# A Fourier mixing layer and an ELU feed-forward on one core: Z on two partition ranges, weights cast by their transfers, bias by matmul, three PSUM tiles for X

## The chip, the core and the metric

The kernel runs on one core of a Trainium2 chip. The core has a matrix engine, TensorE (PE in the profile; its weight loads are shown as PEld), and three engines for elementwise work: VectorE (DVE), ScalarE (ACT) and GpSimd (POOL). SyncE (SP) issues transfers; GpSimd issues some too. TensorE reads SBUF, the on-chip memory with 128 partitions, and writes PSUM, of which there are eight banks of 128 partitions by 512 f32. The other engines move results from PSUM to SBUF ("evict" them). Transfers between SBUF and DRAM run on 16 DMA engines that all queues share.

The metric is the device time of one execution in microseconds (us), as the median of several runs. Before the change it is 906.97 us, with runs from 906.8 to 907.77.

## What is computed

Shapes: x is 8 x 3008 x 256 (batch, sequence, features), w_r and w_i are 256 x 256, moe_w_in is 256 x 2048, moe_w_out is 2048 x 256; all are f32.

```python
X = np.fft.rfft(x, axis=1)
Yr = Xr @ w_r - Xi @ w_i + b_r
Yi = Xr @ w_i + Xi @ w_r + b_i
Yr = np.sign(Yr) * np.maximum(np.abs(Yr) - 0.01, 0.0)     # Yi likewise
y = np.fft.irfft(Yr + 1j * Yi, n=3008, axis=1)
h = y.reshape(24064, 256) @ moe_w_in
g = np.where(h > 0, h, np.exp(np.minimum(h, 0)) - 1)
out = g @ moe_w_out
```

## The kernel before

The sequence length is 47 x 64, so each Fourier transform is done in two small ones, as matmuls with tables of sines that the kernel computes itself in its first 22 us. One batch passes through these units:

- **A** (six units, `unit_A`): x times the table M1, two matmuls of 128x512. The result is evicted as bf16 and stored to DRAM (`DA`). All six stores of a batch must be there before any of it is read back.
- **Z** (`load_Z`, L172): DA is read back in another layout, 96 rows (24 x 2 x 2) on partitions 0 to 95, with 32 slots of 256 features in each row. A group is 8 slots. Batch 0 reads its four groups by four transfers; every other batch by two, one of slots 0 to 7 and one of slots 8 to 31.
- **X** (eight units, `unit_X`): unit u takes group u // 2 of the slots and half u % 2 of the features, eight matmuls of 96 columns against the table M2, which has one set of 96 rows for each slot. The result is evicted into XT by L126 (VectorE) or L128 (ScalarE).
- **M** (twelve groups, `m_group`): XT times the weights. wcat_r holds w_r beside w_i, and wcat_s holds -w_i beside w_r, both in bf16. Four matmuls of 128x512 make a group; then comes the bias and the soft threshold. In batch 0 (`first_M`) the groups alternate between two ways: in one, VectorE adds bias_bc (the bias on all partitions) and GpSimd applies the threshold; in the other, an extra matmul of a tile of ones (`busy`) with bias_p puts the bias into PSUM, where bias_p holds the bias as three bf16 pieces in rows 0, 32 and 64, and ScalarE and VectorE apply the threshold.
- **B** (six units) with the table M3, a store to DRAM (`DB`), a read back (`load_Bs`), and **Y** (eight units) with the table M4, which gives yT, the input of the feed-forward.
- The feed-forward: `front` multiplies a block of 512 tokens by w_in_s, ScalarE takes the exponential, VectorE and GpSimd finish the ELU as gT, and `back` multiplies by w_out_r and stores the output.

The order is written out by hand on every engine (`tc.manual_schedule`): the order in the source is the order of the engine's queue, and each engine works strictly through it. After batch 0's start the feed-forward of one batch runs interleaved with the units A to Y of the next two (`plan`). The first ten blocks (`FILL`) use a PSUM layout of their own, and with them run batch 1's last A units and batch 0's last Y units; batch 1's X units follow.

The start of batch 0 is what the change touches. In order:

- Biases: six small transfers (L441) put the two rows of the bias into `brow`, later VectorE and ScalarE split them into the bf16 pieces of bias_p (L747 to L756). Two further transfers spread the bias over all partitions (L666).
- Tables on VectorE and ScalarE: `points`, `phases`, `wraps`, `signs`, `sizes`, `sines` make M2 group by group.
- `idle_pe(n)` issues n matmuls on a tile of ones, whose results nobody reads: 9 at the start, 3 after each A unit, 40 after the last one, one after each X unit.
- Weights: w_r and w_i come in f32 on SP's queue (L657, L658), and GpSimd makes wcat_r and wcat_s by four operations (L659 to L662).
- `gate(Z_of[0][:, 8, 0:1])` is a tiny GpSimd copy that waits for Z's second group. Behind it in GpSimd's queue stand the transfers of batch 1's x (`load_x`, three of 1 MiB) and of half of w_out (1 MiB). A second such gate stands before batch 2's x.
- w_in comes in four f32 quarters on SP's queue (`load_w_in`, L717), into tiles that the feed-forward needs later (`Et`, `osb`). VectorE scales each by 2/S and casts it to bf16 in two halves (`scale_w_in`, L727), between the M units and in the first blocks of FILL.
- PSUM in the A and X stages: two tiles of two banks each (`pre2`) for the units and four of one bank (`pre1`), which the M groups use then.

## Time and profile before

The profile is of one execution on the chip. That execution took 911.15 us; the span from its first to its last instruction is 909.3 us. Its mean granted TensorE clock is 0.993 of full speed.

| what | value |
|---|---|
| median of three runs | 906.97 us (906.8 to 907.77) |
| the profiled execution, its span | 911.15 us, 909.3 us |
| VectorE: eight scalings of w_in (L727) | 5.2 us, 655 ns each |
| VectorE: bias split (L748, L753 to L756) | 3.3 us |
| SP: issues of Z, all batches (L172) | 18 |
| TensorE: X matmuls (L183), 96 rows x 96 columns | 512, 206 ns in the median |
| TensorE: fillers of `idle_pe` in the first 90 us | 70, 20.8 us |
| DMA moved in the whole span | 106.06 MB, 117 GB/s in the mean |

The durations of matmuls overlap, since they are pipelined; how fast they follow one another is read from the count in a stretch of the chain. The granted clock is given by stretches: 1.00 is full speed, 0.50 is half. A wait is put down to the last thing that released the waiting instruction. "Chain of waits" is the chain of work that ended last, followed back from the last instruction, at each step to what released it.

### The profile page before, as it was taken

How to read it: one execution, taken by the hardware profiler on the slowest of the kernel's cores; microseconds unless marked ns; L12 is line 12 of the kernel's file. 1: busy time of each engine (PE TensorE's matmuls, PEld its weight loads, DVE VectorE, ACT ScalarE, POOL GpSimd, SP SyncE). 2: the span in 40 equal slices, each digit the busy share in tenths (PEclk: the TensorE clock that was granted, in tenths of full speed). 3: DMA queues.
4: the chain of work that ended last, by engine and by line, in shares of the span. 5: the costliest groups of instructions: out<-in, count | busy, mean ns of one | idle time of the engine just before them, and what ended most of it. 6: DMA issues, size and time to landing. Idle time of an engine off the chain costs nothing.

```text
span 909.3 us, 17311 instructions
## 1 busy us (share of the span) xinstructions
PE 887.4 (98%) x6664; PEld 654.4 (72%) x6767; DVE 719.7 (79%) x908; ACT 696.1 (77%) x869; POOL 325.1 (36%) x457
## 2 busy tenths in 40 slices
PE   8898999999999999999999999999999999999997
PEld 3467667876678766886678766787667867777776
DVE  8687778887788778897788877888778877778776
ACT  6577778778878778787787788878887877767664
POOL 7552441233321341405404154032332134443665
PEclk9799999999999999999999999999999999999999
DMA  8977225721283214732266032752228011231011
GB/s 270 296 216 237 74 71 157 238 70 48 70 243 128 71 47 136 195 112 76 64 194 200 26 93 60 210 172 62 78 65 237 25 43 51 73 91 48 24 47 47
DMA packets 90655, 106.06 MB, mean 117 GB/s; under 512 B 5302, under 2 KB 81340, under 8 KB 87212
## 3 DMA queue, kind: packets, MB, share of 16 engines
q1 hardware_dynamic: 84316, 77.42, 30.5%
q0 software_dynamic: 5968, 27.26, 9.0%
q8 instruction: 53, 0.87, 0.4%
q10 hardware_dynamic: 288, 0.26, 0.1%
q14 instruction: 30, 0.25, 0.1%
HBM read 55.12 MB, written 49.81 MB: 115 GB/s over the span
## 4 chain that ended last, share of the span: by engine, by line
PE 85%; DVE 4%; ACT 3%; DMA 3%; issue 2%; POOL 1%; SPq 0%; DVEq 0%; ACTq 0%; POOLq 0%
PE ps_o L945 34%; PE hps L871 33%; PE mps L200 9%; PE bps L252 2%; PE yps L420 2%; PE xps L183 2%; PE aps L150 2%; DMA Z<-DA 1%; DVE gT L915 1%; DVE Et L926 1%; ACT Et L889 1%; ACT Et L892 1%; DMA xt<-in_x_dram 1%; ACT Bz L265 1%; DMA Bs<-DB 0%
## 5 line engine op out<-in xcount | busy, mean ns | idle before, releaser
L945 PE MATMUL ps_o<-w_out_r,gT 128*128 128x256 f32 x3008 | 475.3, 301 | 0.7 <-DVE gT L913 0.7
L945 PEld LDWEIGHTS ps_o<-w_out_r,gT 128*128 128x128 f32 x3008 | 402.9, 189 | 49.8 <-DVE osb L957 1.4
L871 PE MATMUL hps<-yT,w_in_s 128*128 128x512 bf16 (+7 forms) x1613 | 371.9, 350 | 5.9 <-DVE gT L913 1.0
L913 DVE SCALAR_TENSOR_TENSOR gT<-Et,hps 128x512 fp32r<-128x512 f32 (+1 forms) x268 | 220.2, 851 | 74.4 <-POOL Et L924 38.1
L915 DVE SCALAR_TENSOR_TENSOR gT<-hps,Et 128x1024 fp32r<-128x1024 f32 x190 | 232.4, 1223 | 14.9
L871 PEld LDWEIGHTS <-w_in_s 128*128 128x128 bf16 x1728 | 141.8, 98 | 129.0 <-issue 21.5
L924 POOL TENSOR_SCALAR Et<-Et 128x512 f32<-128x512 f32 x204 | 121.5, 615 | 230.9 <-ACT Et L887 218.6
L892 ACT ACTIVATE Et<-hps 128x1024 f32<-128x1024 f32 x190 | 195.8, 1031 | 9.7 <-PE hps L871 3.5
L926 DVE TENSOR_SCALAR Et<-Et 128x1024 f32<-128x1024 f32 x190 | 131.5, 692 | 47.9 <-ACT Et L892 40.4
L218 POOL TENSOR_SCALAR clip<-yb 128x512 f32<-128x512 f32 x84 | 51.7, 615 | 314.5 <-DVE yb L210 282.3
L887 ACT ACTIVATE Et<-hps 128x512 f32<-128x512 f32 x182 | 98.9, 595 | 62.4 <-PE hps L871 60.9
L889 ACT ACTIVATE Et<-hps 128x1024 f32<-128x1024 f32 x84 | 86.3, 1027 | 71.5 <-PE hps L871 70.0
L219 POOL TENSOR_TENSOR Y<-yb,clip 128x512 bf16<-128x512 f32 x84 | 107.2, 1277 | 7.0
L890 ACT ACTIVATE Et<-Et 128x1024 f32<-128x1024 f32 x84 | 88.8, 1058 | 2.6
L210 DVE TENSOR_TENSOR yb<-mps,bias_bc 128x512 f32<-128x512 f32 x89 | 61.3, 689 | 37.2 <-PE mps L200 24.8
L128 ACT CAST XT<-xps 128x768 bf16<-128x768 f32 x61 | 48.8, 799 | 17.9 <-PE xps L183 17.9
L200 PE MATMUL mps<-wcat_r,XT 128*128 128x512 bf16 x180 | 56.7, 391 | 0.8 <-ACT Bz L265 0.3
L200 PE MATMUL mps<-wcat_s,XT 128*128 128x512 bf16 x182 | 55.9, 385 | 0.7
L200 PEld LDWEIGHTS <-XT 128*128 128x128 bf16 x384 | 31.2, 99 | 30.9 <-issue 2.7
L128 ACT CAST A<-aps 128x1024 bf16<-128x1024 f32 x42 | 42.5, 1014 | 13.1 <-PE aps L150 11.7
L128 ACT CAST yT<-yps 128x752 bf16<-128x752 f32 x56 | 44.2, 789 | 10.4 <-PE yps L420 10.3
L265 ACT CAST Bz<-bps 128x1024 bf16<-128x1024 f32 x45 | 45.1, 1001 | 2.7 <-PE bps L252 2.7
(146 smaller groups left out, 466.7 us busy)
## 6 DMA issues: line engine op xcount, KB each, us to landing
xt<-in_x_dram POOLq DMA_DIRECT2D x21, 1024.0 KB, 7.1
out_dram<-osb SPq DMA_DIRECT2D x158, 128.0 KB
Bs<-DB SPq DMA_DIRECT2D x30, 384.0 KB
DA<-A SPq DMA_DIRECT2D x20, 512.0 KB
DB<-Bz SPq DMA_DIRECT2D x20, 512.0 KB
Z<-DA SPq DMA_DIRECT2D x7, 1152.0 KB
Z<-DA SPq DMA_DIRECT2D x11, 384.0 KB
xt<-in_x_dram POOLq DMA_DIRECT2D x6, 512.0 KB, 5.9
```

The costliest lines, as they stand in the source:

```text
L128: nc.scalar.copy(dst, src)
L200: nc.tensor.matmul(ps, lhsT=XT[:, dt, c, o : o + P], rhs=wm[:, dt, :], start=(not biased and m == 0 and dt == 0), stop=(m == 1 and dt == 1),)
L219: nc.gpsimd.tensor_tensor(Y_of[b, q][:, i, :], yb, clip[:], ALU.subtract)
L871: nc.tensor.matmul(hps[s][:, c0:c1] if early else hps[:, s, c0:c1], lhsT=w_in_s[:, dt, ft * P : ft * P + P], rhs=yT_of[b][:, dt, t0 : t0 + ...
L887: nc.scalar.activation(E_[:, s], hps[:, s], AF.Exp)
L889: nc.scalar.activation(E_, hps[:], AF.Relu, scale=-1.0)
L892: nc.scalar.activation(E_, hps[:], AF.Exp)
L913: nc.vector.scalar_tensor_tensor(o, e, -1.0, h, ALU.add, ALU.max)
L915: nc.vector.scalar_tensor_tensor(o, h, 0.0, e, ALU.max, ALU.add)
L924: nc.gpsimd.tensor_scalar(E_[s], E_[s], 1.0, 0.0, ALU.min, ALU.max)
L926: nc.vector.tensor_scalar(E_, E_, 1.0, -1.0, ALU.min, ALU.add)
L945: nc.tensor.matmul(po[q][:, i_ % 2, :], lhsT=gT[:, s, i_ * P : i_ * P + P], rhs=w_out_r[:, ft, :], start=(ft == 0 and i_ % 2 == 0), stop=( ...
```

## The change

It has six parts.

- **Z.** One tile Z0 of 128 partitions serves all batches. Groups 0 and 2 lie on partitions 0 to 95 as before, groups 1 and 3 on partitions 32 to 127. The X matmuls of groups 1 and 3 contract over all 128 partitions, of which the lower 32 of Z0 are cleared once (`clear`, ScalarE). M2 and its tables are computed on 128 partitions, with two sets of per-partition columns (`n=2`), one for each range. Every batch reads Z by four transfers, one for each group.
- **Weights.** GpSimd's queue loads w_r and w_i straight into the bf16 tile wcat_r, behind a gate that waits for the last A tile of batch 0; GpSimd makes wcat_s from it by two operations.
- **w_in.** GpSimd's queue loads it whole, 2 MiB, straight into the bf16 tile w_in_s, ahead of batch 1's x. `load_w_in` and `scale_w_in` are gone. The factor 2/S goes into w40 and w41, and with them into M4. The gates wait for Z's fourth group.
- **Bias.** Two transfers load it as 8 x 64, GpSimd makes the three bf16 pieces there, one transfer stores them to DRAM and three load them into rows 0, 32 and 64 of bias_p. A matmul of ones with bias_p gives the bias on all partitions, and ScalarE evicts it as bias_bc between X units 1 and 3.
- **PSUM.** In the A and X stages there are three tiles of two banks and two of one bank; for the M stage the pools are closed and opened again as two and four. Units 2, 4 and 7 of X are evicted by VectorE (before: 1, 4 and 7).
- **Order.** In batch 0 an M group takes both products of the first half of the features before those of the second. `idle_pe` after the last A unit is 34 matmuls instead of 40, and three instead of eight in the X stage. w3's subtraction moves behind X unit 2, a3 behind X unit 7.

The diff, cut to its core:

```diff
-    M2 = constp.tile([2 * NR, NS, 2, 2 * K1], BF16, name="M2")
+    M2 = constp.tile([P, NS, 2, 2 * K1], BF16, name="M2")
...
-    pre2 = first.enter_context(tc.tile_pool(name="pre2", bufs=2, space=bass.MemoryType.PSUM))
-    pre1 = first.enter_context(tc.tile_pool(name="pre1", bufs=4, space=bass.MemoryType.PSUM))
+    pre2 = zeroth.enter_context(tc.tile_pool(name="pre3", bufs=3, space=bass.MemoryType.PSUM))
+    pre1 = zeroth.enter_context(tc.tile_pool(name="pre0", bufs=2, space=bass.MemoryType.PSUM))
...
-        nc.sync.dma_start(Z_of[b][:, s0:s1, :], dv[:, s0:s1, :])
+        for g in range(s0 // 8, s1 // 8):
+            r, gs = 32 * (g % 2), slice(8 * g, 8 * g + 8)
+            nc.sync.dma_start(Z0[r : r + 2 * NR, gs, :], dv[:, gs, :])
...
+            r = slice(0, P if g % 2 else 2 * NR)
             nc.tensor.matmul(
-                psv[:, kk, 0 : 4 * K1], lhsT=Z[:, k, dt * P : dt * P + P],
-                rhs=M2[:, k].rearrange("p c m -> p (c m)"), start=True, stop=True,
+                psv[:, kk, 0 : 4 * K1], lhsT=Z[r, k, dt * P : dt * P + P],
+                rhs=M2[r, k].rearrange("p c m -> p (c m)"), start=True, stop=True,
             )
...
+        todo = [(c, dt) for c in range(2) for dt in range(2)]
+        if b == 0:
+            todo.sort(key=lambda z: z[1])
...
+    def gate(src):
+        t = gatep.tile([P, 1], F32, name="gate", tag="gate")
+        nc.gpsimd.tensor_copy(t[0 : src.shape[0], :], src)
...
+        def clear(g):
+            nc.scalar.activation(
+                Z0[0:32, 8 * g : 8 * g + 8, :].rearrange("p s d -> p (s d)"),
+                busy[0:32, 0:1].to_broadcast([32, 8 * D]), AF.Copy, scale=0.0,
+            )
...
+        for k in range(3):
+            pool.tensor_copy(bps[:, k], bsm[:])
+            if k < 2:
+                pool.tensor_tensor(bsm[:], bsm[:], bps[:, k], ALU.subtract)
...
-        wc = col(pool, wn, 1.0, ALU.add)
+        wc = col(pool, wn, 1.0, ALU.add, 2.0 / S, ALU.mult)
...
-        nc.sync.dma_start(w_r_f[:], w_r.rearrange("(c p) e -> p c e", p=P))
-        nc.sync.dma_start(w_i_f[:], w_i.rearrange("(c p) e -> p c e", p=P))
-        pool.tensor_copy(wcat_r[:, :, 0:D], w_r_f[:])
-        pool.tensor_copy(wcat_r[:, :, D : 2 * D], w_i_f[:])
-        pool.tensor_scalar(wcat_s[:, :, 0:D], w_i_f[:], -1.0, None, ALU.mult)
-        pool.tensor_copy(wcat_s[:, :, D : 2 * D], w_r_f[:])
+        gate(A_of[0, 2][:, 7, 0:1])
+        for o, wv in ((0, w_r), (D, w_i)):
+            nc.gpsimd.dma_start(
+                wcat_r[:, :, o : o + D], wv.rearrange("(c p) e -> p c e", p=P)
+            )
+        pool.tensor_copy(wcat_s[:, :, D : 2 * D], wcat_r[:, :, 0:D])
+        pool.tensor_scalar(wcat_s[:, :, 0:D], wcat_r[:, :, D : 2 * D], -1.0, None, ALU.mult)
+        for k in range(3):
+            nc.sync.dma_start(bias_p[32 * k : 32 * k + 1, :], bpd[k : k + 1, :])
...
-        idle_pe(40)
+        idle_pe(34)
...
-    load_w_in(0)
-    gate(Z_of[0][:, 8, 0:1])
+    gate(Z_of[0][:, 28, 0:1])
+    nc.gpsimd.dma_start(w_in_s[:], w_in_v)
     for ci in range(3):
         load_x(1, ci)
     load_w_out(0)
...
-    nc.vector.tensor_tensor(rest[:], brow[:], bias_p[:], ALU.subtract)
+    nb = pre1.tile([P, 512], F32, name="ips", tag="mps1")
     for u in range(8):
-        unit_X(0, u, alone=True, on_dve=u in (1, 4, 7))
+        unit_X(0, u, alone=True, on_dve=u in (2, 4, 7))
+        if u == 0:
+            nc.tensor.matmul(nb[:], lhsT=busy[:, 0:P], rhs=bias_p[:], start=True, stop=True)
         if u == 1:
-            nc.scalar.activation(a3[:], w3[:], AF.Abs)
-            nc.vector.tensor_copy(bias_p[32:64], rest[32:64])
-            nc.vector.tensor_copy(bias_p[64:P], rest[64:P])
-            nc.vector.tensor_tensor(rest[64:P], rest[64:P], bias_p[64:P], ALU.subtract)
-            nc.vector.tensor_copy(bias_p[64:P], rest[64:P])
-        idle_pe(1)
+            nc.scalar.copy(bias_bc[:], nb[:])
+        if u == 2:
+            nc.vector.tensor_tensor(w3[:], v3[:], w3[:], ALU.subtract)
+        if u in (1, 3, 5):
+            idle_pe(1)
+    nc.scalar.activation(a3[:], w3[:], AF.Abs)
+    zeroth.close()
...
-    scale_w_in(0, True, 0)
...
-            f1[xs[0]].append((lambda: gate(Z_of[1][:, 16, 0:1]), ()))
+            f1[xs[0]].append((lambda: gate(Z_of[1][:, 28, 0:1]), ()))
```

## The prediction

> **What bounds the kernel now.** I read the page first: its busy rows and its chain by engine.

> ```profile
> span 909.3 us, 17311 instructions
> PE 887.4 (98%) x6664; PEld 654.4 (72%) x6767; DVE 719.7 (79%) x908; ACT 696.1 (77%) x869; POOL 325.1 (36%) x457
> PE 85%; DVE 4%; ACT 3%; DMA 3%; issue 2%; POOL 1%; SPq 0%; DVEq 0%; ACTq 0%; POOLq 0%
> ```

> The matmuls set the end. From about 84 us on they run without a gap worth naming, so the eight batches behind the start cost what they cost, and a change of the start is passed to the end one for one. That leaves the first 84 us, which I read as the chain of waits from 20 to 40 us (start, length, what):

> ```profile
> 22.14 0.86 DVE A L745
> ...
> 23.90 1.10 DVE yb L748
> 25.00 0.88 DVE XT L126
> ...
> 25.92 0.68 PE xps L183 x8
> ...
> 28.77 0.81 ACT XT L128
> ...
> 31.53 0.97 DVE XT L126
> 32.55 1.46 PE mps L200 x3
> ...
> 34.23 2.94 PE mps L200 x8
> 37.16 0.22 PE mps L197
> 37.38 1.73 PE mps L200 x8
> ```

> VectorE is late, not the transfers: the second X unit waited for its eviction at 25.00 because the bias split (L748) stood ahead of it, and with two PSUM tiles the fourth unit waited behind it until 25.92. The same eight M matmuls that take 2.94 us at 34.23 take 1.73 at 37.38. The view by stretches says why (start:end, length, then busy time and count of PE, weight loads, VectorE, ScalarE, GpSimd; granted clock, DMA share, GB/s):

> ```profile
> 19.30:22.70 3.40, 3.40 (x24) 1.69 (x22) 3.37 (x8) 2.07 (x5) 3.40 (x3) 1.00 0.92 253
> 22.70:26.10 3.40, 1.64 (x28) 1.19 (x26) 3.33 (x5) 2.33 (x3) 3.34 (x5) 1.00 1.02 253
> 26.10:29.50 3.40, 3.06 (x27) 2.04 (x25) 2.98 (x5) 1.52 (x2) 1.86 (x3) 0.50 1.07 345
> 29.50:32.90 3.40, 3.07 (x20) 1.67 (x20) 1.34 (x2) 2.44 (x4) 0.00 (x0) 0.50 1.05 414
> 32.90:36.30 3.40, 3.18 (x8) 1.21 (x8) 2.13 (x3) 0.12 (x1) 1.39 (x2) 0.50 1.08 405
> 77.30:80.70 3.40, 2.39 (x27) 1.92 (x26) 1.23 (x3) 1.86 (x3) 0.00 (x0) 1.00 1.01 258
> ```

> After a stretch in which the matmuls were busy 1.64 of 3.40 us the clock is half for 10.2 us; a stretch with 2.39 of 3.40 did not cost it. Last, the timeline where the second batch's Z arrives (the bracket is the engine's idle time and what ended it):

> ```profile
> 77.11 0.52 PE L183 MATMUL xps<-M,Z 96*128 96x96 bf16 x8 [0.40 <-DMA Z<-DA]
> 83.63 0.52 PE L183 MATMUL xps<-M,Z 96*128 96x96 bf16 x8 [0.95 <-DMA Z<-DA]
> ```

> **The X stage: bias off VectorE, a third PSUM tile.** Removed from VectorE between 23.9 and 28.2: L748 1.10, L753 0.42, L754 0.42, L755 0.69, L756 0.70, 3.33 us in all. Added: one matmul (0.22 us, the step of L197 on the chain) and one ScalarE eviction of 128x512 f32 (0.59, the row of L957). The eviction of unit 1 moves to ScalarE, of unit 2 to VectorE. Laid out by the rows (a unit 0.50 at full clock, ScalarE 0.80, VectorE 0.95, Z's groups 1.4 us apart as 22.28 and 23.70 were): unit 1 evicted by 24.6, bias by 25.2, unit 2 on VectorE 24.3 to 25.3, w3 (0.96) to 26.2, unit 4 to 27.2, units 6 and 7 on PE by 27.7, unit 7 evicted at 28.75. First M matmuls 28.0 for the half of XT that is there (the new order), the rest from 28.8, instead of 31.7 and 32.5.

> In the stretch of 22.7 to 26.1 the matmuls then have units 0 to 4, the bias and one filler, some 2.6 of 3.4 us, above the 2.39 that kept the clock; with 34 instead of 40 fillers (0.226 each) the stretch before falls from 3.40 to about 2.5, also above. I take full clock. Then M runs at 0.86 a group and 1.08 with bias: (3,0) to 29.2, (3,1) to 30.3, (4,0) to 31.1, so (4,1) begins at 31.1 where it began at 37.0. One thing holds back: M3 needs a3 (0.84), two sines (0.85, 0.93) and two VectorE steps (0.96, 0.95), with an add of 0.69 between, done at 31.9, and Y(3,1) at 33.4 when B(3) could start at 33.1. **Term: 37.0 - 31.1 - 0.4 = 5.5 us**, about 3 of it waits and 2.5 clock.

> [...]

> **w_in by a casting transfer.** Removed: four SP transfers and eight scalings (L727, 8 x 0.655 = 5.2 us on VectorE). Two stand on the chain of waits, 0.55 at 44.34 and 0.69 at 61.55; the others lie beside the matmuls. **Term: 1.2 us.** Added: one transfer of 2 MiB on GpSimd's queue, ahead of x(1) and half of w_out, and a gate that opens at Z's fourth group instead of its second, 1 us later. Before, 4.5 MiB after the gate took from 24.5 to 38.9, 3.1 us a MiB with the rest of Z; 6 MiB so take 18.5 us, to about 44. Needed: first x tile at 46.5, w_out at 51.5 (51.99 and 56.98 less 5.5), so this is covered by 7 us; without cover each late us is one lost. What it meets: the last DB store (about 40) and the Bs load (48.41 less 5.5). The Bs data was there at 51.1, used at 52.5, 1.4 us of cover. I put 0 to 1.5 us and **take 0.5 lost**. No row shows a cast: nearest are x's transfers (7.3 us for 1 MiB to landing, all at the read's bytes) and, far off, the stretch 19 to 20 us, where the 1 KB rows of w_r and w_i moved 84 GB/s. I take the first, as these are 8 KB rows; the other is the rival on the other side.

> **w_r, w_i and the bias pieces on GpSimd.** GpSimd gains five ops of 8x64 (0.19 to 0.58 by L632 and L458; I take 1.2 us together, 2.9 at most), a gate and two issues (0.68 each), and loses two casts. Its issue of w_r moves from 15.48 (SP) to about 16.6, beside Z's first bytes: Z later by 0 to 1 us, **taken as 0.3**. wcat_s then costs 0.6 to 3.1 an op (L659 to L662), done by 20.5 to 27 against M at 28; at the top ends the gate behind it in the queue opens at 29, which eats 3.5 of the 7 us cover. SP's bpd store stands ahead of two DA stores, but its data is ready near 12 and the fifth store goes at 14.2: nothing. The three bias_p loads take the place of two weight loads (1.0 us of SP), while SP waits for DA until 18.4.

> **Edits at nothing.** Two clears of 32x2048 on ScalarE (0.8 to 2.0 each by L128's 128x768 and 128x1024): the first pushes the sine at 3.76 by 0.5 at most, covered by VectorE's 0.85 us idle ahead of 12.86; the second ends before A at 6.85. Two memsets (0.10) ahead of x's first issue: **0.2 lost**. M2 on 128 instead of 96 rows and a contraction of 128: same columns, same time (weight loads 98 ns for 96 and 128 rows alike in the rows). Fourteen more Z issues on SP (0.4 each, 18 becomes 32): SP waits 295 us for osb alone.

> **Batch 1's Z.** 1152 KB in one piece landed at 83.63, 6.5 us behind the first; as three, the second group lands near 79.3 at the same rate, before unit 2 could start (82.7). **Term: 0.95 us**, 0 at least if the pieces share their bytes, 1.3 at most with unit 0's wait.

> **Sum.** 5.5 + 1.2 + 0.95 - 0.5 - 0.3 - 0.2 = 6.65 us. The profiled execution took 911.15 us (span 909.3 and 1.85 around it), so 904.5 there; it stands 4.2 us above the median of the runs, 906.97, which gives 900.3.

> **Rivals.** (1) *Half clock anyway*, 0.20: X and M are dense sooner, but the clock falls near 26.1 and returns near 36.3. Units 6 and 7 then end at 28.1 (0.85 each), (3,0) at 29.9, (3,1) at 32.1, (4,0) at 33.8, (4,1) near 35.9, where before it ended at 38.1: 2.2 us instead of 5.5, sum 3.35, 903.6 us. For it: the dense stretches 26.1 to 32.9 did not bring the clock back. Against: 2.39 busy kept it.
> (2) *The gain is caught by the Bs chain*, 0.12: M ends early, but DB stores and Bs share the transfers' engines with w_in, x and w_out until 44 and past. If each of three steps (last store, Bs, its use) loses 1.5 us, 4.5 - 1.4 of cover = 3.1 more is lost beside the 0.5: 903.4. Against: 40 to 50 us has a DMA share of 0.51.
> (3) *A slow cast*, slower than before, 0.09: at 84 GB/s w_in takes 25 us instead of 6.2, w_out lands at 63 instead of 51.5, the first ps_o waits 11.3 us, net 11.3 - 6.65 = 4.7 worse: 911.7. It decides from 14 us for w_in (stall begins) and loses on the whole from 21 us, 100 GB/s.
> (4) *No more than the VectorE work*, 0.06: Z comes later than laid out (no gap of 1.4 us) and the X stage ends at 32 as now: only 1.2 us and noise, 905.8 to 907.

> **How the numbers follow.** My forecast has 0.53. Its own range is 898.5 (Z's wait at its top, contention none) to 902.3. 0.2% is 1.8 us, about what a measurement of this kernel can tell from no change. Faster: 0.53 + 0.20 + 0.12 = 0.85, less 0.02 for the far ends of (1) and (2); same 0.07; slower 0.10. The range 897.5 to 906.0 leaves out (3) and the tails.

> **What would show it.** Right: granted clock 1.00 in all stretches from 19 to 40 us; first XT eviction after 24.3 on VectorE without L748 ahead; M matmuls from 28; no PE wait for Z in units 2 and 3 of batch 1; FILL some 6 us earlier; the tail from there of equal length. Wrong: a clock of 0.50 between 26 and 36, PE waiting for w_in_s, xt or w_out_r, or Bs landing later than its use.

## The result, and the profile after

The changed kernel takes 912.83 us in the median (910.8 to 913.5), beside 907.66 us (906.8 to 908.13) for the kernel before on the same chip. The ratio is 1.0056 with a 95% interval of 1.0043 to 1.0069: slower by 0.56%, about 5.1 us. The forecast was 900.3 us, in a range from 897.5 to 906.0.

The profiled execution took 912.54 us. First the busy rows and the chain by engine of its page:

```profile
span 910.8 us, 17287 instructions
...
PE 883.6 (97%) x6654; PEld 652.8 (72%) x6757; DVE 712.2 (78%) x896; ACT 700.4 (77%) x871; POOL 325.7 (36%) x466
...
PE 86%; DVE 3%; issue 3%; ACT 3%; POOL 2%; DMA 2%; SPq 0%; DVEq 0%; ACTq 0%; POOLq 0%
```

VectorE lost its 7.5 us of work (719.7 before) and TensorE 3.8 us, and the span still grew. So something waits that did not. The chain of waits from 18 to 62 us shows where (start, length, what):

```profile
18.33 9.11 DMA wcat_r<-in_w_i_dram
...
27.52 1.53 POOL wcat_s L696
...
33.41 1.27 POOL Y L243
34.69 0.04 issue
34.73 0.61 PE bps L256 x8
...
47.91 0.66 PE lateA L301 x2
48.57 5.93 issue
54.51 1.41 PE one L397 x16
```

Up to 29 us it is w_i's transfer, 9.1 us from its issue to landing, and GpSimd's work behind it. At 48.57 stands the loss: TensorE is idle for 5.93 us ahead of the first Y matmul, which reads Bs. "issue" says that the chain found no releaser; the waits of SP's and GpSimd's queues between 40 and 56 us name it (us in total, times, longest):

```profile
SPq L289 <- DMA DB<-Bz: 9.1, 1, 9.1
...
POOL gate L450 <- DMA Bs<-DB: 10.8, 1, 10.8
```

SP waits 9.1 us for batch 0's last DB store before it may issue the Bs load. The view by stretches (start:end, length, busy time and count of PE, weight loads, VectorE, ScalarE, GpSimd; granted clock, DMA share, GB/s), first over the X and M stages, then over the hole:

```profile
22.70:26.10 3.40, 1.85 (x36) 1.42 (x35) 1.84 (x3) 2.51 (x4) 0.70 (x1) 1.00 1.08 255
26.10:29.50 3.40, 2.19 (x28) 1.23 (x26) 2.03 (x3) 2.72 (x4) 1.98 (x3) 1.00 0.06 10
29.50:32.90 3.40, 3.35 (x16) 1.56 (x16) 3.02 (x5) 3.05 (x5) 3.40 (x6) 1.00 0.72 93
...
49.00:53.00 4.00, 0.00 (x0) 0.00 (x0) 0.00 (x0) 0.00 (x0) 0.00 (x0) 1.00 0.41 103
...
55.00:57.00 2.00, 2.00 (x21) 1.26 (x19) 1.74 (x4) 1.51 (x4) 0.98 (x1) 0.50 0.23 35
```

Three things are to be seen. The clock stays full from 22.7 to 32.9 us. From 26.1 to 29.5 us the transfers' engines do nothing (share 0.06; before it was 1.07): Z has landed, and GpSimd, held by w_i, has not yet issued w_in. What they did not move then they move from 29 to 50 us, when the DB stores want them too. And from 49 to 53 us no engine computes, after which the matmuls run at half clock for some 6 us more.

How the stores were held up is read from the DMA view by queue (packets, MB, share of 16 engines). q0 is GpSimd's queue (w_in, x, w_out), q1 SP's (DB stores, Bs). After, 38 to 40 us and 44 to 46 us:

```profile
q0 software_dynamic: 120, 0.85, 106.8%
q1 hardware_dynamic: 3, 0.00, 0.4%
```

```profile
q0 software_dynamic: 329, 0.44, 75.7%
q1 hardware_dynamic: 332, 0.16, 41.3%
```

The first store is issued at 36.4 us. By 40 us the stores have got three packets. From 40 to 48 us the two queues move nearly the same number of packets, 106 to 102, 91 to 93, 329 to 332, 410 to 413 in each 2 us, but a DB packet has some 0.5 KB (0.21 MB in 413 from 46 to 48 us), one of x some 8 KB (104 of q0's 120 from 38 to 40 us have that or more), one of w_out 1 KB (0.42 MB in 410 from 46 to 48 us). So SP's queue got 0.05 MB of 0.80 in each 2 us from 40 to 44 us, and a quarter to a third of the bytes behind that. Why they got only three before 40 us is not shown.

Last, batch 1's X units in the timeline, where the third one had waited 0.95 us for Z (the first and the third are shown):

```profile
79.81 0.52 PE L185 MATMUL xps<-M,Z 96*128 96x96 bf16 x8 [0.36 <-DMA Z<-DA]
...
85.26 0.52 PE L185 MATMUL xps<-M,Z 128*128 128x96 bf16 x8
```

### The profile page after: what moved, and what is told of

Its sections match the earlier page's. It is cut to its first block, busy times and chain, and to the rows that moved or that the text cites. A ratio compares the mean times of both kernels' runs of the same rounds, so it can differ in the third digit from the quotient of the medians.

```text
span 910.8 us, 17287 instructions
## 1 busy us (share of the span) xinstructions
PE 883.6 (97%) x6654; PEld 652.8 (72%) x6757; DVE 712.2 (78%) x896; ACT 700.4 (77%) x871; POOL 325.7 (36%) x466
## 4 chain that ended last, share of the span: by engine, by line
PE 86%; DVE 3%; issue 3%; ACT 3%; POOL 2%; DMA 2%; SPq 0%; DVEq 0%; ACTq 0%; POOLq 0%
PE ps_o L951 35%; PE hps L877 33%; PE mps L204 9%; PE bps L256 2%; PE yps L424 2%; PE aps L150 2%; PE xps L185 2%; DMA wcat_r<-in_w_i_dram 1%; PE sps L877 1%; DVE gT L921 1%; DVE Et L932 1%; ACT Et L898 1%; ACT Et L895 1%; ACT Bz L269 1%; POOL xt L117 1%
## 5 line engine op out<-in xcount | busy, mean ns | idle before, releaser
L951 PEld LDWEIGHTS ps_o<-w_out_r,gT 128*128 128x128 f32 x3008 | 403.2, 189 | 48.7 <-DVE osb L963 1.3
L214 DVE TENSOR_TENSOR yb<-mps,bias_bc 128x512 f32<-128x512 f32 x89 | 61.3, 688 | 36.3 <-PE mps L204 22.7
L128 ACT CAST XT<-xps 128x768 bf16<-128x768 f32 x61 | 48.7, 800 | 14.8 <-PE xps L185 14.8
L204 PEld LDWEIGHTS <-XT 128*128 128x128 bf16 x384 | 30.8, 98 | 29.8 <-ACT XT L128 0.7
L128 ACT CAST yT<-yps 128x752 bf16<-128x752 f32 x56 | 44.2, 789 | 9.7 <-PE yps L424 9.6
L128 ACT CAST A<-aps 128x1024 bf16<-128x1024 f32 x42 | 42.5, 1014 | 11.4 <-PE aps L150 10.4
```

The source lines that it names most:

```text
L128: nc.scalar.copy(dst, src)
L204: nc.tensor.matmul(ps, lhsT=XT[:, dt, c, o : o + P], rhs=(wcat_r, wcat_s)[c][:, dt, :], start=(not biased and (c, dt) == (0, 0)), stop=((c ...
L951: nc.tensor.matmul(po[q][:, i_ % 2, :], lhsT=gT[:, s, i_ * P : i_ * P + P], rhs=w_out_r[:, ft, :], start=(ft == 0 and i_ % 2 == 0), stop=( ...
```

## The experiments

Each ratio is to runs of the kernel before on the same chip. "Bs issued" is the moment when SP issues batch 0's Bs load, which is when the last DB store that it needs has landed. The last three columns come from one profiled execution of each kernel; those of e3 (910.19 us) and e6 (908.40 us) are the slowest of their ten runs.

| kernel | median, us | ratio (95%) | gate on Z opens | Bs issued | first Y matmul |
|---|---|---|---|---|---|
| before, as profiled first | 906.97 (this one 911.15) | | 24.5 | 48.4 | 52.6 |
| e1: before, profiled again | 907.06 | 0.9998 (0.9988 to 1.0008) | 25.2 | 45.2 | 48.7 |
| after | 912.83 | 1.0056 (1.0043 to 1.0069) | 29.0 | 51.6 | 54.5 |
| e2: after, w_out behind Bs | 911.41 | 1.0039 (1.0024 to 1.0053) | 28.6 | 48.4 | 51.2 |
| e3: after, w_in as before | 908.49 | 1.0008 (0.9998 to 1.0017) | 30.3 | 49.0 | 52.7 |
| e4: after, w_r and w_i as before | 911.25 | 1.0038 (1.0023 to 1.0053) | 27.4 | 50.6 | 53.4 |
| e5: after, 2 MiB moved behind Bs | 908.37 | 1.0017 (1.0007 to 1.0026) | 27.7 | 45.8 | 48.6 |
| e6: e5 and e4 together | 906.94 | 1.0000 (0.9990 to 1.0009) | 28.0 | 46.5 | 49.4 |
| e7: before, w_in cast | 907.87 | 1.0009 (1.0000 to 1.0019) | 25.5 | 47.8 | 50.6 |
| e9: before, Z's part | 908.02 | 1.0007 (0.9999 to 1.0016) | 24.7 | 46.9 | 50.4 |
| e10: before, bias, PSUM, order | 907.04 | 1.0002 (0.9993 to 1.0012) | 25.3 | 45.7 | 49.5 |
| e11: after, w_in, w_r, w_i as before | 906.83 | 0.9997 (0.9988 to 1.0005) | 27.8 | 46.4 | 49.3 |
| e12: e4, w_in cast in quarters | 910.59 | 1.0037 (1.0024 to 1.0050) | 27.1 | 46.9 | 49.7 |
| e13: e11, gate at second group | 906.47 | 0.9990 (0.9982 to 0.9999) | 24.7 | 45.4 | 48.4 |
| e14: e4, gate at second group | 906.90 | 1.0002 (0.9993 to 1.0011) | 24.7 | 47.4 | 50.3 |
| e15: after, early gate | 906.88 | 0.9999 (0.9990 to 1.0008) | 24.9 | 47.1 | 50.0 |

The theory was that w_in's bytes and the late gate on GpSimd's queue starve the DB stores, and with them Bs and TensorE. The rivals were a starvation that would only move elsewhere, and a loss in the Z, bias or PSUM parts.

### e1: the kernel before, once more

No edit.

> The kernel before, profiled a second time, because its profiled execution took 911.15 us and the median of its runs is 907. If the profiled execution was an ordinary one slowed by the profiler alone, this profile again shows a granted clock of 0.50 for about 10 us between 26 and 37 us, and the time is 907 to 908 with a profile near 911. If the half clock is what set that execution apart, this profile shows a clock of 1.00 in the X and M stages, a span near 905, and the part of my 5.5 us that was clock (about 2.5 us) was never there to gain in the median.

Its profiled execution took 906.76 us. The stretches of it that stood in the prediction at 1.64 busy and then half clock:

```profile
22.70:26.10 3.40, 2.40 (x36) 1.70 (x36) 3.32 (x6) 2.22 (x3) 3.00 (x4) 1.00 1.02 255
26.10:29.50 3.40, 2.72 (x38) 1.78 (x36) 2.43 (x5) 2.19 (x4) 2.63 (x4) 1.00 1.07 300
29.50:32.90 3.40, 2.90 (x12) 1.19 (x13) 3.35 (x4) 2.25 (x4) 0.74 (x1) 1.00 1.06 417
```

Full clock throughout; (4,1) begins at 33.12 us instead of 37.0, and batch 1's first M matmul, from which on the matmuls run steadily, stands at 92.3 instead of 96.5. In the first profile the fourth X unit had waited 1.66 us:

```profile
25.92 0.68 PE L183 MATMUL xps<-M,Z 96*128 96x96 bf16 x8 [1.66 <-DVE XT L126]
```

Here it waits 0.33 us. The 4.2 us by which the first profile stood above its median went with this wait and the half clock behind it. Every comparison of places below is with e1. Its DMA view by queue, 38 to 40 and 42 to 44 us, also shows what the changed kernel lacks, and so does SP's wait for the stores from 40 to 46 us:

```profile
q0 software_dynamic: 527, 0.52, 143.7%
q1 hardware_dynamic: 306, 0.16, 28.4%
```

```profile
q1 hardware_dynamic: 811, 0.41, 68.4%
```

```profile
SPq L285 <- DMA DB<-Bz: 2.6, 2, 2.0
```

GpSimd's queue is empty soon after 40 us (17 packets from 40 to 42 us, none from 42 to 44), and the DB stores share the engines only with SP's own w_in quarter.

### e2: w_out's first half behind the Bs load

```diff
-    load_w_out(0)
...
     gate(Bs_of[0, 0][64:96, 0, 0:1])
+    load_w_out(0)
     load_w_out(1)
```

> The changed kernel, only that the first half of w_out is issued behind the Bs gate with the second half. Theory (the DB stores of batch 0 hardly move while GpSimd's queue moves w_in, x and w_out, so Bs is late): GpSimd's queue is empty near 45 instead of 51 us, Bs lands near 50 instead of 54.5, the first Y matmuls start near 50, and the time falls by 4 to 6 us to about 907 to 909. Rival (the wait is not of that traffic, but of the tables, the PSUM pools or the late gate): first Y stays near 54 and the time at 912 or above. Rival (the weights themselves are late): w_out now lands near 54 or later, PE waits for it, and the time does not fall.

Measured 911.41 us. The chain of waits:

```profile
42.34 5.90 DMA DB<-Bz
...
51.64 6.41 DMA w_out_r<-in_moe_w_out_dram
```

The last store landed 3.2 us sooner with 1 MiB less ahead, as the theory says. But then TensorE waited 3.4 us for the 1 MiB that had been moved. The gain of 1.4 us is all that is left; x and w_in still held the stores for 5.9 us.

### e3 and e4: one half of GpSimd's new load undone

e3 takes w_in back to four f32 quarters on SP's queue with VectorE's eight casts; the factor stays in M4. e4 takes w_r and w_i back:

```diff
-        gate(A_of[0, 2][:, 7, 0:1])
-        for o, wv in ((0, w_r), (D, w_i)):
-            nc.gpsimd.dma_start(
-                wcat_r[:, :, o : o + D], wv.rearrange("(c p) e -> p c e", p=P)
-            )
-        pool.tensor_copy(wcat_s[:, :, D : 2 * D], wcat_r[:, :, 0:D])
-        pool.tensor_scalar(wcat_s[:, :, 0:D], wcat_r[:, :, D : 2 * D], -1.0, None, ALU.mult)
+        nc.sync.dma_start(w_r_f[:], w_r.rearrange("(c p) e -> p c e", p=P))
+        nc.sync.dma_start(w_i_f[:], w_i.rearrange("(c p) e -> p c e", p=P))
+        pool.tensor_copy(wcat_r[:, :, 0:D], w_r_f[:])
+        pool.tensor_copy(wcat_r[:, :, D : 2 * D], w_i_f[:])
+        pool.tensor_scalar(wcat_s[:, :, 0:D], w_i_f[:], -1.0, None, ALU.mult)
+        pool.tensor_copy(wcat_s[:, :, D : 2 * D], w_r_f[:])
```

> The changed kernel, with w_in alone loaded and cast as before (four f32 quarters on SP's queue, eight VectorE casts). Theory: GpSimd's queue carries 4 MiB instead of 6 and is empty near 40, before the last DB store is issued; Bs lands near 47, no wait of more than 1 us ahead of the first Y matmuls, no half clock there; FILL pays the casts again (about 1.2 us); time 903 to 906. Rival (Z's new place, the casting loads of w_r and w_i or the bias make the loss): 911 to 913 stays.

> The changed kernel, with w_r and w_i alone loaded by SP in f32 and cast by GpSimd as before. Theory: the gate behind wcat_s in GpSimd's queue opens near 27.2 (when Z's last group lands) instead of 29.0, all of GpSimd's transfers end about 2 us earlier, Bs lands near 52.5, time 910 to 911. Rival (the late w_i is the main cause): the wait ahead of the first Y matmuls goes and the time falls below 907.

Without w_in's cast 4.3 of the 5.1 us come back (908.49 us). With w_r and w_i as before 1.6 us come back (911.25 us): the gate opened at 27.4 instead of 29.0 us and Bs was there 1.1 us sooner. In e3's profile Z was late:

```profile
25.92 0.82 PE L185 MATMUL xps<-M,Z 96*128 96x96 bf16 x8 [3.89 <-DMA Z<-DA]
```

TensorE waited 3.89 us for Z, and its eight X matmuls then took 0.82 instead of 0.52 us; why Z was late is not shown. This start, and not the DB stores, makes e3's first Y late in the table: SP waited 2.6 us for the stores and TensorE not at all ahead of Y. As it is the slowest of ten runs, it shows what can happen there and not what the median pays.

### e5 and e6: the second half of w_in and x's third tile behind the Bs load

```diff
-    nc.gpsimd.dma_start(w_in_s[:], w_in_v)
-    for ci in range(3):
+    HF = DFF // 2
+    nc.gpsimd.dma_start(w_in_s[:, :, 0:HF], w_in_v[:, :, 0:HF])
+    for ci in range(2):
         load_x(1, ci)
...
     gate(Bs_of[0, 0][64:96, 0, 0:1])
+    nc.gpsimd.dma_start(w_in_s[:, :, HF:DFF], w_in_v[:, :, HF:DFF])
+    load_x(1, 2)
     load_w_out(1)
```

e6 has e4's edit as well.

> The changed kernel, with w_in loaded in two column halves, and the second half together with batch 1's third x tile put behind the Bs gate, ahead of the second half of w_out. Theory (DB's stores are starved by whatever GpSimd's queue still has to move when they are issued, 36 to 42 us): 4 MiB instead of 6 stand ahead, the queue is empty near 40, the last DB store lands near 45 instead of 51.5, Bs near 47.5, the first Y matmuls start near 48.5 as in the kernel before, and FILL goes without the eight scalings; time 904 to 907. Rival (x's third tile or half of w_in are then late for FILL, or the starvation moves to batch 1's DA stores): 908 or more, with PE waiting for xt or w_in_s, or Z later.

> As the run before in this list (w_in in halves, late part behind the Bs gate), and w_r and w_i loaded by SP and cast by GpSimd as in the kernel before. Theory: the gate opens at Z's landing near 27.4 instead of 29, GpSimd's queue is empty near 38.5, which is now well ahead of the last DB store, so nothing or up to 0.5 us more is gained; 904 to 906.5. Rival (the gate's delay is what counts): 1.5 us or more better than that run.

e5: 908.37 us, e6: 906.94 us. With 2 MiB less ahead of them the stores of e5 landed by 45.8 us and the first Y matmul ran at 48.6, as in e1: the starvation at that place is gone. But from `front(0)` to batch 1's first X unit it took 25.6 us instead of e1's 23.6, and the chain of waits of e5 has this piece:

```profile
62.02 7.04 DMA Bs<-DB
```

That is batch 0's second Bs load, now beside the 2 MiB that had been moved and w_out's second half. So the rival was half right: the loss moves with the bytes, at a lower price. e6 is 1.4 us faster than e5, close to its rival's 1.5, though its gate opened no sooner; what makes the difference is not shown.

### e7, e9 and e10: one part alone, on the kernel before

e7 has only w_in's cast (gate at the second group, as it was); e9 only Z's part (the tile Z0, M2 on 128 rows, four transfers); e10 only the bias by matmul, the three PSUM tiles and the order.

```diff
     gate(Z_of[0][:, 8, 0:1])
+    nc.gpsimd.dma_start(w_in_s[:], w_in_v)
     for ci in range(3):
```

> The kernel before, with the casting load of w_in alone (whole, ahead of batch 1's x; the eight scalings gone, 2/S in the last table). Theory: the gate opens near 25 as it did, 6 MiB last to about 44.5, the last DB store (issued near 42) is held to then, Bs lands near 50 instead of 47.9, 2 us lost and 1.2 us of scalings gained: 907 to 909. Rival (the loss needs no late gate; w_in alone bears it): 911 or more. Rival (w_in's load is harmless and the loss came from elsewhere): 905 to 906.

> Z's part alone on the kernel before: odd groups on partitions 32 to 127, M2 on 128 rows, the clears, one piece per group. My sum: batch 1's second X unit pair no longer waits for Z, 0.95 us gained there, so about 906.3 us beside about 907.2 for the kernel before; first X matmul and last DB store as before (23 and 45 us). Rival (the pieces share their bytes, or the wait was hidden work's slack): no gain, 906.8 to 907.7, and the stretch from batch 1's first X unit to the first steady M stays 18.6 us instead of about 17.7.

> The kernel before, with the X stage's part alone: bias pieces on GpSimd and through DRAM, bias by matmul, three PSUM tiles, the new order of M's products, 34 and 3 fillers. Theory (in an ordinary execution the clock stays full in X and M, so only the waits were there to gain): the bias matmul of (4,1) at 31.5 to 32 instead of 33.1, 1.2 to 1.6 us less, 905.5 to 906.2. Rival (the 5.5 us of my prediction): 902. Rival (Z's arrival is the bound, nothing is gained): 907.

None of the three is worth more than 0.1% either way. e7 loses what the theory gives it: the stores landed 2.6 us later than in e1 and the first Y matmul ran 1.8 us later, of which 0.4 us is left at the first steady M matmul (92.66 against 92.28). With an early gate the cast costs little. e9 missed its 0.95 us: from batch 1's first X unit to the first steady M it took 18.1 instead of 18.6 us, but the first M matmul stood at 31.2 instead of 29.8, since VectorE came to its last tables 1.4 us later (L718 at 22.40, in e1 at 21.00) and the bias split ahead of its second eviction was later with them. The delay begins early. Three operations on the per-partition columns, now two wide, take 1.72 (for two of them) and 0.95 us at 4.73 and 6.76, where e1's take 0.34 and 0.15, and the tables behind them begin 1.7 us later (8.29 instead of 6.60). The changed kernel has the same rows (1.72 and 0.95 us). Why they are slow is open. e10 gained nothing at all. In its profile (4,1) began at 33.96, not at the expected 31.5 to 32: the first X unit ran 0.5 us later than in e1 (23.85), and the clock in the stretches of the prediction was:

```profile
26.10:29.50 3.40, 2.19 (x35) 1.56 (x35) 2.80 (x4) 2.69 (x5) 2.54 (x4) 1.00 0.97 283
29.50:32.90 3.40, 3.40 (x9) 1.19 (x10) 2.46 (x4) 2.21 (x3) 0.33 (x1) 0.51 1.00 381
```

The clock was half for 3.4 us, behind a stretch with 2.19 busy, the same 2.19 that left the clock full in the changed kernel.

### e11: everything heavy taken off GpSimd's queue

The edits of e3 and e4 together; Z, bias, PSUM and order stay as changed.

> The changed kernel with w_in (quarters on SP, scaled by VectorE) and w_r, w_i (SP, GpSimd casts) as before; Z, bias and PSUM parts stay. Theory (the whole loss is the load on GpSimd's queue): last DB store issued work done as before, Bs load issued by 46 us, no half clock, 906 to 907.5 us. Rival (the Z and X parts cost something of their own, as the 908.49 us with w_in alone undone might say): 908 us or more with Bs issued before 46. By my sum without w_in's term the X and Z parts should still give 2.4 us (1.44 plus 0.95): 904.9.

906.83 us, ratio 0.9997. The whole loss is gone with w_in, w_r and w_i, and the rival that the Z and X parts make a loss falls. So does the sum's 904.9: the parts that should have gained 2.4 us gained nothing that shows. The gate opened at 27.8 us, and Bs was issued 1.25 us later than in e1.

### e12: w_in in quarters

e4 with w_in cast in four pieces, one at the old place, three behind the Bs load.

```diff
     gate(Bs_of[0, 0][64:96, 0, 0:1])
+    load_w_in(1)
     load_w_out(1)
+    load_w_in(2)
+    load_w_in(3)
```

> The changed kernel with w_r, w_i as before and w_in cast in quarters: the first where the whole stood, the second behind Bs's gate ahead of w_out's second half, the last two behind that. Early bytes on GpSimd's queue are again 4.5 MiB. Theory: Bs load issued by 46 us, and the late pieces cost less of the fill than the 1 MiB half did: 905.5 to 907 us. Rival (any late piece starves batch 0's remaining Bs loads, packet by packet): the stretch from front(0) to batch 1's first X unit is 25 us instead of 23.6 and the time 907 to 908.5, or PE waits for w_in_s.

910.59 us, worse than either theory expected. The Bs load was issued at 46.85 us, 0.85 later than expected, and the clock was at 0.57 from 50 to 54 us; then TensorE needed the second quarter, as the chain and the timeline show:

```profile
51.88 9.55 DMA w_in_s<-in_moe_w_in_dram
```

```profile
61.48 0.82 PE L887 MATMUL sps<-yT,w_in_s 128*128 128x512 bf16 x3 [2.14 <-DMA w_in_s<-in_moe_w_in_dram]
```

512 KB took 9.55 us there, beside w_out and Bs, where the whole 2 MiB took 8.0 us in the changed kernel. The rival came in both branches: the wait for w_in_s, and 24.9 us from `front(0)` to batch 1's first X unit.

### e13, e14 and e15: the gate alone

```diff
-    gate(Z_of[0][:, 28, 0:1])
+    gate(Z_of[0][:, 8, 0:1])
```

on e11 (e13) and on e4 (e14). e15 is the whole change with this edit, and with gate and w_in's issue ahead of the two operations that make wcat_s:

```diff
-    gate(Z_of[0][:, 28, 0:1])
+    gate(Z_of[0][:, 8, 0:1])
     nc.gpsimd.dma_start(w_in_s[:], w_in_v)
+    nc.gpsimd.tensor_copy(wcat_s[:, :, D : 2 * D], wcat_r[:, :, 0:D])
+    nc.gpsimd.tensor_scalar(wcat_s[:, :, 0:D], wcat_r[:, :, D : 2 * D], -1.0, None, ALU.mult)
```

> The kernel of e11 (Z, bias and PSUM parts kept, w_in, w_r and w_i as before) with GpSimd's gate put back to Z's second group. e11's gate opened at 27.8 instead of 25.2 us and its Bs load was issued at 46.4 instead of 45.15, which by the theory ate what the X stage had gained. Theory: gate near 25.5, Bs issued by 45, first Y matmul by 48.5, and with batch 1's 0.8 us kept 905.5 to 906.5 us, ratio about 0.9985. Rival (the early start of x holds Z's third and fourth group back by as much): X units wait for Z, first M 1 us later than e11's 29.1, and 906.8 us as e11.

> The kernel of e4 (whole change but w_r, w_i as before) with the gate put back to Z's second group. If the late gate is what makes w_in dear (the transfers' engines stood at a share of 0.10 and 0.39 from 26 to 30 us in e4): gate near 25, no hole from 26 to 30, Bs load issued by 48, as in the kernel with w_in alone (47.75), and 907 to 908 us, ratio 1.000 to 1.001. If the extra 1.5 MiB on the queue is the cause by itself: Bs issued near 50 and 910 us or more, as e4 with its 911.25 (1.0038).

> The whole change with two moves on GpSimd: the gate at Z's second group, and gate and w_in's issue ahead of the two wcat_s operations, which wait for w_i until 27.4. If the hole in the transfers from 26 to 30 us is the price: w_in issued near 25.5, Bs issued by 48.5, 908 to 909 us. If w_in then meets w_i and Z instead (M waits for wcat_s past 31): a gain of under 1.5 us on the changed kernel, 911 us or more.

906.47, 906.90 and 906.88 us. e15 settles the cause of the loss: the changed kernel with these lines in another order is level with the kernel before (0.9999), better than its own expectation. It does not win, since its first Y matmul is still 1.3 us behind e1's (50.01 against 48.73) and the blocks behind it give 1.1 us back. The stretches from 26 to 28 and 28 to 30 us, of e4 and then of e14, show what the edit does (columns as above):

```profile
26.00:28.00 2.00, 1.54 (x25) 1.16 (x26) 2.00 (x3) 1.35 (x3) 0.29 (x2) 1.00 0.10 29
28.00:30.00 2.00, 1.48 (x12) 0.67 (x12) 0.97 (x2) 2.00 (x4) 2.00 (x4) 1.00 0.39 27
```

```profile
26.00:28.00 2.00, 1.58 (x25) 1.16 (x26) 1.92 (x3) 1.04 (x2) 2.00 (x4) 1.00 0.81 119
28.00:30.00 2.00, 1.41 (x12) 0.65 (x12) 0.96 (x1) 2.00 (x4) 0.75 (x1) 1.00 1.03 203
```

The hole in the transfers is filled (share 0.10 and 0.39, then 0.81 and 1.03). The four kernels with the Z and X parts make a table of two by two:

| | gate at the fourth group | gate at the second |
|---|---|---|
| w_in as before | 0.9997 (e11) | 0.9990 (e13) |
| w_in cast whole | 1.0038 (e4) | 1.0002 (e14) |

The late gate alone costs 0.07%, the cast alone 0.12%, both together 0.48%. The first two differences lie within the intervals (0.08 to 0.15% to either side), the third does not: neither the bytes nor the gate is the cause by itself. In the profiles the late gate delays the Bs load by 1.0 us without the cast (45.4 to 46.4) and by 3.2 us with it (47.4 to 50.6). Only e4 then has a long gap ahead of Y (5.02 us; 1.80 in e14), and its mean granted clock is 0.996 (0.998 in e13, 0.999 in e11 and e14). From the first Y matmul to the first ps_o it needs 6.45 us, the other three 4.4, so by estimate about 2 us of its loss are clock. Why the two delays more than add up is not shown. w_r and w_i on the same queue add 0.18% (e4 to the changed kernel), where the gate opens at 29.0 instead of 27.4 us. e13 is the one kernel of all that is faster than the one before, by 0.1% with an interval that almost touches 1 (0.9982 to 0.9999).

## Why the prediction was wrong

**The step that failed: "covered by 7 us ... take 0.5 lost".** The sum found that GpSimd's queue would be busy until about 44 us and held that against x and w_out, which indeed came in time: no wait for w_out in the changed kernel, and w_in landed 8.0 us after its issue. It did not hold it against SP's queue, whose DB stores are issued from 36.4 to 42 us and which lay inside that time by the prediction's own numbers. The collision was named, "the last DB store (about 40) and the Bs load", and priced at 0 to 1.5 us from the cover of 1.4 us; the runs show a wait of 9.1 us for the stores (2.6 in e1), 5.8 us at the first Y matmul (54.51 against e1's 48.73), and 1.6 us more by the first ps_o, the output of `back`, from the half clock behind it. The blocks up to batch 1's X units gave 1.3 us back (19.2 instead of 20.5 us) and batch 1's X stage 0.3, which leaves 5.8 us at the first steady M matmul (98.11 against 92.28) and between the two executions (912.54 and 906.76).

**The gate's time.** "1 us later", to about 25.5, was taken; it opened at 29.01. The text did say that at the top ends it would open at 29, and charged this to the same cover. e15 shows that this lateness is what the whole result hangs on. The term for the weights, 0.3 us for Z, looked at the wrong victim: w_i's packets moved beside Z's (138 of q1 to 113 of q0 from 23 to 25 us), and it was w_i that came late (9.11 us).

**The 5.5 us of the X stage.** The places came out near those laid out: M began at 28.43 us (28.0), (4,1) at 31.68 (31.1), the clock was full. But the comparison was with one execution. In e1 (4,1) begins at 33.12, so 1.44 us of the 5.5 were there to be had. Even these were not the X stage's: the changed kernel's first X unit ran at 21.87 and e1's at 23.33, and from there to (4,1) both needed 9.8 us (e4 and e13, with w_r and w_i loaded as before, 8.7). In the changed kernel units 4 and 6 of X waited 0.78 and 0.39 us for Z. Nor does its start secure the clock: e2, which has the same code up to there, lost it from 26.1 to 29.5 us (0.51). Then the half clock of the profiled execution, and the wait ahead of it, were counted twice: once as a gain, and once in the 4.2 us between that execution and the median. The prediction had both numbers and did not connect them.

**"0.4 for M3 and Y(3,1)".** Even the 1.44 us did not arrive: B(3) began at 34.73 instead of 35.15. The row before it was missed. Y(3,0) is GpSimd's, and its add on VectorE stands behind M3's first step: in the changed kernel that add runs at 30.76, the clip at 32.44 (0.88) and Y from 33.41 to 34.67. In e13, where GpSimd had nothing to issue then, Y still ended at 34.45. The chain of sines, add, clip and Y sets B(3) there: B(3) waits 0.94 us for Y in the changed kernel, 0.56 in e11 and 0.45 in e13, and not at all in e1. In e11 and e13 it began 0.3 and 0.65 us before e1's, which is all that the earlier X and M work brought in these profiles.

**The small terms.** The scalings' 1.2 us were there: from the first ps_o to batch 1's first X unit e11 and e13 needed 20.5 and 20.6 us, and e4 and e14, which differ from them by w_in's cast, 19.4 and 19.3. Batch 1's Z: the third unit's wait, 0.95 us in the first profile but 0.64 in e1, is gone in every kernel with the Z part; it is also gone in e7, which does not have it. From batch 1's first X unit to its first M the kernels with the Z part needed 17.7 to 18.5 us where e1 needed 18.6 and e7 17.4, so no run isolates this term. Memsets: nothing seen. What the list of edits at nothing left out is the columns two wide on VectorE: the tables behind them begin 1.7 us late (e9).

**The rivals.** "The gain is caught by the Bs chain" had the right mechanism; its price, three steps of 1.5 us, was a guess at a queue that in fact got 1/16 of the bytes from 40 to 44 us, and "40 to 50 us has a DMA share of 0.51", held against it, was read from a kernel whose GpSimd queue is empty by then. At the measured price it is a loss and not a smaller gain. "A slow cast" falls: from 32.9 to 36.3 us the changed kernel wrote 212 GB/s of bf16 at a share of 1.06, which is 424 GB/s read, the 425 of x in e1. "Half clock anyway" did not happen in the changed kernel's profile where it was placed, though it did in e2's; there B(3) still began at 35.14 us, as in e1.

## What to carry to other kernels

When a transfer is put on a queue ahead of others, work out when that queue runs empty, and hold this against every transfer of every other queue that is issued before then, not only against the one that stands behind it; in the changed kernel the queue of small packets moved as many as the other (102 and 106 from 40 to 42 us) and little of the bytes (0.05 of 0.80 MB). The late gate left the transfers idle first (a share of 0.06 from 26.1 to 29.5 us) and crowded them later (1.05 to 1.31 from 36 to 50 us), so look for the hole in the DMA row as well as for the wait. And when the profiled execution stands off the median by more than the runs scatter, find what is odd in it before taking a term from it.
